# A reciprocal root on GpSimd, three chunks turned through DRAM, and a first tile on two queues

## The chip, the cores and the metric

The kernel runs on one core of one Trainium2 chip. Five engines work side by side in a core: TensorE (PE: matmuls and transposes, which write the PSUM banks; its weight loads are shown as PEld), VectorE (DVE), ScalarE (ACT), GpSimd (POOL) and SyncE (SP, which here issues the DMAs). Each engine takes its own instructions in order, and semaphores tie them together. The metric is the device time of one launch in microseconds.

## The reference

The input x is 2048 rows of 640 columns. Two parts follow each other, each with a layer norm ahead and a residual sum behind:

```python
def _layernorm(x, axis=-1, eps=1e-5):
    m = jnp.mean(x, axis=axis, keepdims=True)
    v = jnp.var(x, axis=axis, keepdims=True)
    return (x - m) / jnp.sqrt(v + eps)

h = x + _A_ref(_layernorm(x, axis=-1), A_wqkv, A_wo)
h2 = h + _B_ref(_layernorm(h, axis=-1), B_w_gate, B_w_up, B_w_down)
```

`_A_ref` is an attention with 32 heads of 20 columns in which every position sees itself and seven earlier ones at a distance of 2, 4, ... 14: `x @ wqkv` (640 x 1920), softmax over the 8 logits, the weighted sum of values, then `@ wo` (640 x 640). `_B_ref` is `(silu(x @ w_gate) * (x @ w_up)) @ w_down` with 1728 inner columns.

## The kernel before, in words

**Tiling.** The rows are taken in 4 blocks of 512, each held as 128 partitions by 4 row groups (`j`) of 640 columns. Every float32 matrix is split into a high part in the matmul's reduced type and a low remainder, and each product is made of three passes (high by high, high by low, low by high). So each operand costs an ACT copy for the high part and a VectorE subtraction for the low one.

**Stages.** `ln1` normalises a block's rows and turns them into columns, `qkv` multiplies them by the attention weights (480 columns at a time, four groups `g`) and writes queries, keys and values to DRAM; the scale of each row is applied as ACT empties the bank (L585). `att_load`, `att_qk`, `att_exp` and `att_av` do the attention of one block and group, nearly all of it on VectorE (L629, L636, L664, L672), and send the turned output to DRAM. `wo` multiplies by the output weights (L827), adds x and takes the second norm's statistics; `ln2_columns` turns the rows again (for blocks 0 to 2 the first half through DRAM, in `turn_pair`, and the second by TensorE, in `pair_columns`, L447 to L450). `ffn` runs 14 chunks of the feed-forward weights for blocks 0 and 1: `load_ffn` brings the weights into one of two raw buffers, `proj` (L899) makes gate and up, `gate` the product, `down` (L910) adds into five banks. Blocks 2 and 3 share some of their products (`early`, `pair`, `closing`; L994). The stages overlap: matmuls of one block run while VectorE does the attention of another.

**The norm's deviation.** `LnStats.rstd(j, n)` turns variances into 1/sqrt(var + eps) for n row groups at once. ACT takes the square root (L410; this needs another function table than the exponential and the silu, and a load of it shows as ACT_TABLE_LOAD), and VectorE makes the reciprocal and one Newton step in five or six instructions on 1 to 4 columns (L403 to L409, the last one makes the row bias). It is called 14 times: four times for block 0's first norm, once for each of the other three, twice for the second norm of blocks 0, 1 and 2, and once for that of block 3. `apply` and `apply_pair` then scale the rows on ACT.

**The end of a block.** `finish` adds the five banks of the down product to the rows and stores them. Four banks hold columns 0 to 511 of one row group each. The fifth holds columns 512 to 639 of all four row groups, the wrong way round: ACT copies it out (L1197), TensorE turns it in four transposes (L1201), VectorE adds it (L1212). It is called five times: for blocks 0 and 1, for block 2's first part (not stored), for block 3, and for block 2's second part at the very end.

**The start.** SP loads row groups of block 0's x one at a time (L514) and the attention weights (L553) in the planner's order. TensorE runs ten filler matmuls (`warm`, L497) from the start. For each row group VectorE takes mean and variance and subtracts the mean (`one_dve`, L390 to L392), TensorE turns it in five transposes (L541), and ACT and VectorE split it.

**The order.** Nothing is issued where it stands in the code. `P.add(engine, cost, function, reads, writes, priority)` collects some 2,700 operations, each of one or several instructions. `Plan.order` lists them by estimated costs and priorities (`PR`), then again in several rounds (`ROUNDS`) by due times that follow from TensorE's order. At the end the estimated start of each operation, plus a correction by its number (`SHIFT`), is the key of a last topological sort, and the functions are called in that order. The numbers of operations shift when operations are added or removed.

**On GpSimd** run a few memsets and, for 12 of the 16 attention groups, one sum (L690 and L692), of which the first instruction is there to wait: it reads the product that VectorE's L629 writes, so that the large sum starts when VectorE begins the one-input reduction L636.

Of the kernel before, what the change touches and what calls it, by code (L numbers as in the profile page):

```python
# [10 lines left out]
F32 = mybir.dt.float32  # L11
# [14 lines left out]
LOADED = (1, 2)  # L26
TURN = (3,)
# [3 lines left out]
EPS = 1e-5  # L31
# [5 lines left out]
ROUNDS = ((1.0, 20, 1.5), (1.5, 10, 3.5), (1.1, 0, 1.5), (1.4, 20, 3.5), (1.3, 3, 2.5), (1.2, 3, 2.5), (1.3, 20, 5.0),)  # L37
PR = {'g1': 0.6, 'y1': 0.6, 'x': 0.5, 'yst': 8, 'yld': 2, 'wqd': 4, 'wqh': 0.5, 'wql': 4, 'qev': 1, 'kvs': 0.4, 'atl': 1.2, 'exp': 0.5, 'ost': 3, 'wod': 2, 'woh': 8, 'wol': 1.2, 'old': 1.5, 'fld': 4, 'lst': 6, 'wev': 1.5, 'fh': 2.2, 'fl': 8, 'ln1': 8, 't1': 1, 'wo0': 1.2, 'wo': 2.2, 'ln1t': 1.2, 'xb': 0.4, 'tr': 10, 't1t': 2.2, 'ln1d': 0.5, 'hst': 10, 'hld': 10, 'ht': 1, 'hc': 2, 'jd': 3, 'jp': 8, 'js': 4, 'jl': 0.4, 'ja': 0.5, 'jfld': 1.2, 'jfh': 4, 'jfl': 1, 'jhi': 4, 'jmu': 0.4, 'jlo': 0.9, 'jcm': 0.5, 'w3': 1, 'w3e': 8, 'w3o': 0.4, 'w3x': 8, 'w3l': 2.2, 'jy': 6}

SHIFT = {  # L40
# [161 lines left out]
def program(tc, x_in, wqkv_in, wo_in, ffn_in, ffl_in, const_in, out):  # L202
# [7 lines left out]
    with tc.tile_pool(name="sb", bufs=1) as sb, tc.tile_pool(  # L210
# [51 lines left out]
        zsc = dr.tile([NB, D, 4, 64], F32, name="zsc")  # L262
        msc = dr.tile([6, 2, 128, 512], F32, name="msc")
# [19 lines left out]
        EPSC, BN, MV, RS1 = LN + 120, LN + 80, LN + 92, LN + 100  # L283
# [5 lines left out]
        def f(o, n):  # L289
            return fa[:, o : o + n]  # L290
# [16 lines left out]
        P.add("DVE", 0.2, lambda: V.memset(f(EPSC, 1), EPS), w=[rf(EPSC, 1)], prio=0)  # L307
        P.add("ACT", 0.1, lambda: A.activation(f(LN + 119, 1), f(EPSC, 1), AF.Sqrt), r=[rf(EPSC, 1)], w=[rf(LN + 119, 1)], prio=0, table="sqrt")
# [15 lines left out]
        class LnStats:  # L324
# [41 lines left out]
            def apply_pair(self, j):  # L366
                o = lambda: f(XN, 1280).rearrange("p (f j t) -> p f j t", j=2, t=32)[:, :, j, :]
                P.add("ACT", 0.95, lambda: A.activation(o(), self.src(j).rearrange("p (f t) -> p f t", t=32), AF.Identity, bias=f(self.NB + j, 1), scale=f(self.RS + j, 1)),
                      r=[self.srcr(j), rf(self.NB + j, 1), rf(self.RS + j, 1)], w=[rf(XN, 1280)], prio=self.prio)

            def one_bn(self, j):
# [9 lines left out]
                P.add("DVE", 1.45, bn, r=[self.srcr(j)], w=[rf(BN, 12), rf(MV + 2 * j, 2), rf(self.NEG + j, 1)], prio=self.prio)  # L381

# [12 lines left out]
            def rstd(self, j, n, after=()):  # L395
                STD, RS, TM, NEG, NB = (o + j for o in (self.STD, self.RS, self.TM, self.NEG, self.NB))
# [3 lines left out]
                fold = self.RS == self.SUM + 16  # L400

                def newton():
                    V.tensor_scalar(f(TM, n), var, sc, EPS, op0=ALU.mult, op1=ALU.add)  # L403
# [4 lines left out]
                    if fold:  # L408
                        V.tensor_mul(f(NB, n), f(NEG, n), f(RS, n))  # L409
# [966 lines left out]
```

## Time and profile before

| | |
|---|---|
| median of 3 runs | 844.13 us (843.86 to 844.89) |
| the profiled execution's own time | 841.39 us |
| its span, first to last instruction | 839.3 us |
| granted TensorE clock, mean | 0.999 |
| TensorE busy | 831.4 us, 99% of the span |
| VectorE busy | 694.7 us, 83% |
| ACT busy | 414.0 us, 49% |
| GpSimd busy | 23.2 us, 3% |

The profile is one execution. Its page gives busy times of the engines; further views give them by stretches of time, by groups of instructions (line, engine, operation, out<-in, shapes, count, then busy time and mean ns of one, then the idle time ahead of them and what ended it), the list of who waited for whom, the chain of work that ended last, and the instructions in order of time (start in us, length in us, then the instruction). In the latter, a mark in brackets is the engine's idle time before the instruction and what ended it. In rows of DMA issues the last number is the median time from issue to landing. "SPq" is SP's queue issuing a DMA.

### The profile page before, as it was taken

Reading aid. Unit: us, or ns where it says so; the run is one execution under the profiler, and the core shown is the slowest. Engines: PE = TensorE matmul, PEld = TensorE weight load, DVE = VectorE, ACT = ScalarE, POOL = GpSimd, SP = SyncE. Lnnn points to the kernel's source line nnn. Section 1 sums busy time; section 2 is a strip of 40 time slices with the busy share of each in tenths; the row PEclk is TensorE's granted clock in tenths of the full one; section 3 lists DMA queues with packets and bytes.
Section 4 is the critical chain, followed back from the end, with each engine's and each line's share of the span. In section 5 each row is a group of like instructions: output and inputs, shape, how many; then the busy total and the mean of one; then the engine's idle time right before and its main releaser. Section 6 shows DMA issues by size and latency. Waiting matters only on the chain.

```text
span 839.3 us, 10718 instructions
## 1 busy us (share of the span) xinstructions
PE 831.4 (99%) x3903; PEld 705.0 (84%) x3903; DVE 694.7 (83%) x823; ACT 414.0 (49%) x694; POOL 23.2 (3%) x33
## 2 busy tenths in 40 slices
PE   8999999999999999999999999999999999999998
PEld 7888888889978889888888988888887888888886
DVE  8599999999999999999999999996327866655552
ACT  7755853333763445755443486464465533323231
POOL 0000000000000000000000000000000000000000
PEclk9999999999999999999999999999999999999999
DMA  8996786568688687669898658787587644454441
GB/s 265 331 367 219 284 272 216 185 213 307 197 304 263 224 289 258 212 210 372 287 365 289 233 174 304 250 269 268 156 264 270 218 170 137 136 169 144 154 133 71
DMA packets 101796, 198.32 MB, mean 236 GB/s; under 512 B 35744, under 2 KB 61152, under 8 KB 101104
## 3 DMA queue, kind: packets, MB, share of 16 engines
q1 hardware_dynamic: 101744, 197.65, 69.6%
q8 instruction: 30, 0.49, 0.2%
q14 instruction: 22, 0.18, 0.1%
HBM read 147.87 MB, written 49.75 MB: 235 GB/s over the span
## 4 chain that ended last, share of the span: by engine, by line
PE 75%; DVE 15%; DMA 4%; issue 2%; ACT 2%; SPq 1%; DVEq 0%; ACTq 0%
PE bank L580 20%; PE bank L910 17%; PE bank L899 17%; PE bank L994 16%; PE bank L827 5%; DVE fa L629 2%; DVE fa L636 2%; DVE fa L672 2%; DVE fa L664 2%; DMA fa<-ysc 1%; DMA fa<-in_ffn_dram 1%; DMA ysc<-fa 1%; DVE fa L934 1%; DMA fa<-in_wqkv_dram 1%; DMA fa<-osc 1%
## 5 line engine op out<-in xcount | busy, mean ns | idle before, releaser
L899 PE MATMUL bank<-shb,ra 128*128 128x512 f32 x810 | 189.7, 390 | 1.1 <-DVE shb L450 1.1
L899 PEld LDWEIGHTS bank<-shb,ra 128*128 128x128 f32 x810 | 151.4, 188 | 32.4 <-DVE shb L450 1.5
L910 PE MATMUL bank<-ra,acts 128*128 128x512 f32 (+1 forms) x662 | 161.9, 389 | 0.2 <-DVE acts L945 0.2
L910 PEld LDWEIGHTS bank<-ra,acts 128*128 128x128 f32 x662 | 122.6, 188 | 25.5 <-DVE acts L945 0.5
L580 PE MATMUL bank<-ra,sha 128*128 128x480 f32 x480 | 105.1, 379 | 0.6 <-ACT sha L543 0.6
L580 PE MATMUL bank<-ra,shb 128*128 128x480 f32 x470 | 102.5, 378 | 0.0
L580 PEld LDWEIGHTS bank<-ra,sha 128*128 128x128 f32 x480 | 89.8, 188 | 14.5 <-ACT sha L543 0.9
L580 PEld LDWEIGHTS bank<-ra,shb 128*128 128x128 f32 x470 | 88.1, 188 | 13.2
L664 DVE TENSOR_TENSOR fa<-fa 128x2560 f32<-128x2560 f32 x32 | 90.2, 2820 | 0.6
L629 DVE TENSOR_TENSOR fa<-fa 128x2560 f32<-128x2560 f32 x32 | 90.1, 2816 | 0.8 <-DMA fa<-ksc 0.4
L636 DVE TENSOR_REDUCE fa<-fa 128x128 f32<-128x2560 f32 x32 | 90.0, 2814 | 0.4
L994 PE MATMUL bank<-shb,ra 128*128 128x512 f32 x360 | 86.8, 390 | 0.3 <-DVE fa L938 0.3
L1137 DVE TENSOR_TENSOR fa<-bank,fa 128x512 f32<-128x512 f32 x60 | 41.1, 691 | 52.8 <-PE bank L994 51.4
L994 PEld LDWEIGHTS bank<-shb,ra 128*128 128x128 f32 x360 | 67.2, 188 | 14.6 <-DVE fa L938 0.7
L672 DVE TENSOR_TENSOR fa<-fa 128x1280 f32<-128x1280 f32 (+2 forms) x70 | 76.7, 1095 | 1.1
L827 PE MATMUL bank<-ra 128*128 128x320 f32 x480 | 75.0, 310 | 0.0
L827 PEld LDWEIGHTS bank<-ra 128*128 128x128 f32 x480 | 72.1, 188 | 2.9 <-ACT fa L830 1.3
L585 ACT ACTIVATE st<-bank,fa 128x480 f32<-128x480 f32 x64 | 41.9, 656 | 57.2 <-PE bank L580 54.4
L994 PE MATMUL bank<-ra 128*128 128x512 f32 x288 | 68.2, 389 | 0.0
L944 ACT CAST acts<-fa 128x512 fp32r<-128x512 f32 x47 | 29.1, 620 | 71.9 <-DVE fa L934 50.3
L994 PEld LDWEIGHTS bank<-ra 128*128 128x128 f32 x288 | 54.1, 188 | 11.2
L876 ACT CAST ra<-fa 128x1280 fp32r<-128x1280 f32 (+1 forms) x38 | 45.8, 1205 | 24.1 <-PE bank L899 15.0
(146 smaller groups left out, 834.5 us busy)
## 6 DMA issues: line engine op xcount, KB each, us to landing
fa<-in_ffn_dram SPq DMA_DIRECT2D x46, 960.0 KB, 6.5
ra<-lsc SPq DMA_DIRECT2D x45, 320.0 KB, 3.0
fa<-ksc SPq DMA_DIRECT2D x16, 880.0 KB, 6.0
fa<-vsc SPq DMA_DIRECT2D x16, 880.0 KB, 6.9
ra<-lsc SPq DMA_DIRECT2D x21, 640.0 KB, 5.0
lsc<-ra SPq DMA_DIRECT2D x13, 640.0 KB, 3.2
ksc<-st SPq DMA_DIRECT2D x16, 320.0 KB, 2.8
qsc<-st SPq DMA_DIRECT2D x16, 320.0 KB, 3.6
```

Of the source, the lines that this page charges most:

```text
L580: T.matmul(banks[bk][:, 0:480], l, r_(wq(g, w, c), 480), start=(p, c) == first_mm, stop=(p, c) == last_mm)
L585: P.add("ACT", act(480) + 0.06, lambda bk=bk, j=j: A.activation(stage_t()[:, so : so + 1920].rearrange("p (t j c) -> p t j c", t=3, j=NJ)[ ...
L629: P.add("DVE", dve(2560), lambda: V.tensor_tensor(f(PROD, 2560).rearrange("p (j w c) -> p j w c", j=2, w=W), window(ko, 2 * jp), f(qo + 32 ...
L636: P.add("DVE", dve(2560), lambda: V.tensor_reduce(f(lo + 128 * jp, 128), f(PROD, 2560).rearrange("p (n d) -> p n d", d=DH), axis=AX.X, op= ...
L664: V.tensor_tensor(f(PROD, 2560).rearrange("p (j w d) -> p j w d", j=2, d=DH), bass.AP(tensor=fa[:, vo : vo + 160].tensor, offset=fa[:, vo ...
L672: V.tensor_add(dst(v), v[:, :, 0:m, :], v[:, :, m : 2 * m, :])
L827: T.matmul(banks[bk][:, 0:320], l, r_(m, 320), start=p == 0 and c == 0, stop=p == 2 and c == NC - 1)
L876: P.add("ACT", act(n), lambda: A.copy(r_(gu, n), f(raw, n)), r=[rf(raw, n)], w=[rr(gu, n)], prio=PR["fh"])
L899: T.matmul(banks[bk], r_(gu + 1280 * w + wid * c + col, 128), x2(a, c), start=p == 0 and c == 0, stop=p == 2 and c == NC - 1)
L910: T.matmul(banks[bk][:, lo:hi], l, m, start=first and p == 0, stop=last and p == len(passes) - 1)
L994: T.matmul(banks[bk], r_(ws[w] + 256 * q, 128), x(a, c), start=start and p == n == q == 0, stop=stop and p == 2 and n == len(terms) - 1 an ...
L1137: dv(0, lambda: V.tensor_add(fb(h, dst), banks[bk], fb(h, src)), [pb(bk)] + fr(h, src), fr(h, dst))
```

## The change

Four things are changed together.

- `rstd` becomes one operation of two GpSimd instructions: variance times a factor plus eps, then that to the power -0.5, whose exponent lies in a column filled by a memset. The square root on ACT, its first table load, and the Newton step on VectorE go. The row bias, minus mean times deviation, is now made on ACT beside each scaled row (`scaled`), 16 times.
- `finish` turns the last chunk of blocks 0, 1 and 3 (`FLAT`) by a VectorE transpose in 32x32 squares, one store to DRAM and four loads that put the squares in place. The unstored call for block 2 copies its chunk to LG as it is, and the last call adds that copy before the turn, which stays with TensorE. The very last row group's stores go out in halves on SP and ACT.
- Block 0's first row group is loaded in two halves, on SP and on ACT. Its mean is summed by ACT (256 columns) and VectorE (384 columns), the mean is subtracted from the first 128 columns and then from the other 512, and the five transposes go as one and four into banks 7 and 6.
- `ROUNDS` has nine rounds in place of seven, and `SHIFT` moves 194 operations (57 before). By the new numbers 10 is the first load of attention weights, 31 and 32 are the two subtractions of the first mean, 34 to 39 the first row group's transposes and splits, and 1008 and 1011 are two of the three subtractions at L450 for block 0.

```diff
-ROUNDS = ((1.0, 20, 1.5), (1.5, 10, 3.5), (1.1, 0, 1.5), (1.4, 20, 3.5), (1.3, 3, 2.5), (1.2, 3, 2.5), (1.3, 20, 5.0),)
+ROUNDS = ((1.5, 10, 3.5), (1.0, 6, 1.5), (1.3, 0, 5.0), (1.3, 6, 3.5), (1.4, 3, 1.5), (1.5, 20, 5.0), (1.2, 10, 1.5), (1.4, 10, 1.5), (1.0, 3, 5.0),)
 SHIFT = {
...
+    0: 12.6, 10: -198.4, 19: 2, 31: -245, 32: -195.6, 33: -1.9, 34: -118.2, 35: -103.5, 36: -91.6, 37: -90.6,
...
+    -0.3, 240: 10.4, 247: 19.9, 255: -2.7, 263: -30.3, 276: -18.9, 285: 9.2, 288: 26.8, 298: -9, 306: 6.9, 313:
...
+    928: 45.4, 932: -5.8, 940: 10.7, 942: -27.6, 958: -25.3, 979: -0.3, 986: -25.8, 1008: -26.1, 1011: -47,
...
-        P.add("DVE", 0.2, lambda: V.memset(f(EPSC, 1), EPS), w=[rf(EPSC, 1)], prio=0)
-        P.add("ACT", 0.1, lambda: A.activation(f(LN + 119, 1), f(EPSC, 1), AF.Sqrt), r=[rf(EPSC, 1)], w=[rf(LN + 119, 1)], prio=0, table="sqrt")
+        P.add("POOL", 0.1, lambda: G.memset(f(POW, 1), -0.5), w=[rf(POW, 1)], prio=0)
...
+            def one_split(self, j, cut=384):
+                src, xo = self.src(j), XN + 640 * j
+                P.add("ACT", 0.6, lambda: A.activation(f(xo + cut, 640 - cut), src[:, cut:640], AF.Identity, accum_out=f(self.SUM + j, 1)),
...
+                def mean():
+                    V.tensor_reduce(f(self.NEG + j, 1), src[:, 0:cut], axis=AX.X, op=ALU.add)
+                    V.tensor_scalar(f(self.NEG + j, 1), f(self.NEG + j, 1), f(self.SUM + j, 1), 1.0 / D, op0=ALU.add, op1=ALU.mult)
...
+                for o, e in ((0, 128), (128, 640)):
+                    P.add("DVE", 0.155 + 0.0006 * (e - o), lambda o=o, e=e: V.tensor_scalar(f(xo + o, e - o), src[:, o:e], f(self.NEG + j, 1), None, op0=ALU.subtract),
...
-                def newton():
-                    V.tensor_scalar(f(TM, n), var, sc, EPS, op0=ALU.mult, op1=ALU.add)
-                    V.reciprocal(f(RS, n), f(STD, n))
...
-                P.add("ACT", 0.3, lambda: A.activation(f(STD, n), var, AF.Sqrt, bias=f(EPSC, 1), scale=sc), r=[vr, rf(EPSC, 1), *after], w=[rf(STD, n)], prio=self.prio, table="sqrt")
...
+                def power():
+                    G.tensor_scalar(f(TM, n), var, sc, EPS, op0=ALU.mult, op1=ALU.add)
+                    G.tensor_tensor(f(RS, n), f(TM, n), f(POW, 1).to_broadcast([128, n]), op=ALU.pow)
+                P.add("POOL", 0.9, power, r=[vr, rf(POW, 1), *after], w=[rf(RS, n), rf(TM, n)], prio=self.prio)
...
+            def scaled(self, j, o, i, w):
+                NEG, RS, NB = (f(q + j, 1) for q in (self.NEG, self.RS, self.NB))
+
+                def rows():
+                    A.mul(NB, NEG, RS)
+                    A.activation(o(), i(), AF.Identity, bias=NB, scale=RS)
...
+            if js == (0,):
+                for a, (eng, E) in enumerate((("SP", Q), ("ACT", A))):
+                    P.add(eng, 0.4, lambda a=a, E=E: E.dma_start(
+                        fa[a:128:2, XR : XR + 640],
+                        x_in[0, 64 * a : 64 * a + 64, 0, :]), w=[("xh", a, a + 1)] if a else [rf(XR, 640)], prio=0, nbytes=nb(64, 2560))
...
-                (st.one_dve if j < 3 else st.one)(j)
-                for c0, n, bk, bo in ((0, 4, 7 - j % 2, 0), (4, 1, 5, j)):
+                (st.one_split if j == 0 else st.one_dve if j < 3 else st.one)(j)
+                for c0, n, bk, bo in ((0, 1, 7, 0), (1, 4, 6, 0)) if j == 0 else ((0, 4, 7 - j % 2, 0), (4, 1, 5, j)):
...
+            so = SIL if b == 2 else AB2 if b < 2 else XN + 2048
+            if not store:
+                P.add("ACT", act(512), lambda: A.copy(f(LG, 512), banks[d4]), r=[pb(d4)], w=[rf(LG, 512)], prio=0)
+            elif b == 2:
+                P.add("DVE", dve(512), lambda: V.tensor_add(f(so, 512), banks[d4], f(LG, 512)), r=[pb(d4), rf(LG, 512)], w=[rf(so, 512)], prio=0)
...
+            if store and b in FLAT:
+                cols, ckey = (lambda: f(so, 512)), rf(so, 512)
+                P.add("DVE", dve(512), lambda: V.transpose(f(so, 512), f(so, 512)), r=[ckey], w=[ckey], prio=PR["dt"])
+                P.add("SP", 0.45, lambda: Q.dma_start(dsc[b], f(so, 512)), r=[ckey], w=[(f"D{b}", 0, 4)], prio=PR["dt"], nbytes=nb(128, 2048))
+                for q in range(4):
+                    P.add("SP", 0.65, lambda q=q: Q.dma_start(
+                        fa[32 * q : 32 * q + 32, so : so + 512].rearrange("t (j d c) -> t j d c", j=NJ, d=4),
+                        dsc[b].rearrange("(d t) (j q c) -> q t j d c", t=32, j=NJ, q=4)[q]),
+                        r=[(f"D{b}", 0, 4)], w=[(f"T{b}", q, q + 1)] if q else [ckey], prio=PR["dt"], nbytes=nb(512, 128))
...
+                    if final and j == NJ - 1:
+                        for a, (eng, E) in enumerate((("SP", Q), ("ACT", A))):
+                            P.add(eng, 0.4, lambda row=row, o=o, e=e, a=a, E=E: E.dma_start(out[b, 64 * a : 64 * a + 64, NJ - 1, o:e], row()[a:128:2]), r=[key], prio=3, nbytes=nb(64, 4 * (e - o)))
```

More of the change, by code (lines that the diff above doesn't have):

```diff
@@ L419, in apply @@
                     i = lambda j: self.src(j).rearrange("p (f t) -> p f t", t=32)
-                P.add("ACT", 0.95, lambda: A.activation(o, i(j), AF.Identity, bias=f(self.NB + j, 1), scale=f(self.RS + j, 1)),
-                      r=[self.srcr(j), rf(self.NB + j, 1), rf(self.RS + j, 1)], w=[rf(XN, 2560) if self.turned else rf(xo, 640)], prio=self.prio)
+                self.scaled(j, lambda: o, lambda: i(j), rf(XN, 2560) if self.turned else rf(xo, 640))
+            def scaled(self, j, o, i, w):
[3 more added lines that the diff above has]
+                    A.activation(o(), i(), AF.Identity, bias=NB, scale=RS)
+                P.add("ACT", 1.2, rows, r=[self.srcr(j), rf(self.NEG + j, 1), rf(self.RS + j, 1)], w=[w, rf(self.NB + j, 1)], prio=self.prio)
         def turn_pair(b):
```

49 lines of the change are left out of this document (26 added, 23 removed), and 24 rows, old and new, of the table SHIFT.

## The prediction

> **What bounds the kernel now.** I read the page's first part, then the busy time by stretches, then the list of who waited for whom on TensorE.
>
> ```profile
> span 839.3 us, 10718 instructions
> PE 831.4 (99%) x3903; PEld 705.0 (84%) x3903; DVE 694.7 (83%) x823; ACT 414.0 (49%) x694; POOL 23.2 (3%) x33
> ```
>
> ```profile
> 0.00:10.00 10.00, 7.60 (x29) 5.77 (x30) 6.75 (x15) 4.96 (x10) 1.17 (x7) 1.00 0.76 249
> 10.00:230.00 220.00, 220.00 (x1063) 193.47 (x1062) 203.54 (x221) 123.06 (x245) 6.88 (x8) 1.00 0.77 260
> 230.00:240.00 10.00, 8.91 (x45) 7.17 (x45) 9.97 (x12) 8.34 (x13) 1.72 (x2) 1.00 0.80 297
> 240.00:830.00 590.00, 589.26 (x2741) 493.92 (x2740) 470.55 (x572) 277.63 (x428) 13.42 (x16) 1.00 0.68 228
> 830.00:839.30 9.30, 5.65 (x31) 4.69 (x30) 3.89 (x7) 0.00 (x0) 0.00 (x0) 0.91 0.36 141
> ```
>
> ```profile
> PE bank L497 <- POOL ra L1239: 1.3, 1, 1.3
> PE bank L899 <- DVE shb L450: 1.1, 1, 1.1
> ```
>
> The columns of the stretches are PE, PEld, DVE, ACT, POOL, then the granted clock. A busy matmul engine need not run at its best, so a second view is wanted, the chain of work in order of time:
>
> ```profile
> 13.86 165.46 PE bank L580 x766
> 254.17 6.80 PE bank L899 x30
> 260.97 3.40 PE bank L910 x15
> ```
>
> The chain has long runs of nothing but matmuls, 0.216 us apart at 480 columns (165.46 / 766) and 0.227 at 512 (6.80 / 30), at a granted clock of 1.00. So TensorE really is the bound. It idles 839.3 - 831.4 = 7.9 us: 2.4 in the first 10, 1.1 where block 0 is handed to the feed-forward stage (L450), 0.7 in the 590 us behind that, and 3.65 at the end. This decides how the parts are priced: work taken from ACT, VectorE or GpSimd is worth nothing unless one of those 7.9 us waits for it; work taken from TensorE is worth its whole length; and a new wait of TensorE costs its whole length, since there are no gaps to take it up.
>
> **The change, part by part.** *The turned chunk.* `finish` is called five times, each with one group of four TensorE transposes (L1201). Three (blocks 0, 1, 3) now turn on VectorE and through DRAM, and one (block 2's first, unstored) keeps its chunk unturned in LG. Four groups go, one stays.
>
> ```profile
> 394.53 0.60 PE L1201 MATMUL bank<-fa 128*128 128x128 f32 x4
> 394.88 0.48 PE L899 MATMUL bank<-shb,ra 128*128 128x512 f32 x1
> 812.64 0.66 PE L1201 MATMUL bank<-fa 128*128 128x128 f32 x4
> 813.05 0.47 PE L910 MATMUL bank<-ra,acts 128*128 128x512 f32 x1
> ```
>
> From the first transpose to the next matmul pass 0.35 and 0.41 us, so four groups are worth 1.4 to 1.6 us: take 1.5. This is the surest term, since matmuls stand on either side.
>
> In their place come, for each of three blocks, a VectorE transpose of 128x512, one store and four loads, all on SP's queue.
>
> ```profile
> L702 DVE STREAM_TRANSPOSE fa<-fa 128x320 f32<-128x320 f32 x30 | 15.2, 505 | 0.1
> L424 DVE STREAM_TRANSPOSE fa<-fa 128x1280 f32<-128x1280 f32 x3 | 4.5, 1503 | 0.9 <-ACT fa L368 0.9
> zsc<-fa SPq DMA_DIRECT2D x12, 160.0 KB, 4.0
> fa<-zsc SPq DMA_DIRECT2D x3, 640.0 KB, 5.8
> fa<-in_ffn_dram SPq DMA_DIRECT2D x46, 960.0 KB, 6.5
> ```
>
> By a line through the two transposes, 512 columns take 0.70 us; three are 2.1 us of VectorE, beside matmuls (the unstored call drops one addition). The DRAM round is 4.0 + 5.8 = 9.8 us by the nearest store and load. Only the last columns' addition and the output stores wait for it, nothing of TensorE. It does hold SP: the four loads wait for the store's landing, and what is queued behind them, weight loads above all, waits too, up to 4.0 us for each block. A weight load lands after 6.5 us, and a chunk of weights feeds TensorE for 6.80 + 3.40 = 10.2 us with two buffers in turn; that cover of 3.7 us and more hides most of the 4.0. I cost it at nothing; without the cover it would be three times up to 4.0, that is 12.0. In the block 3 case it runs within the last 25 us, where the output must only land before the end.
>
> *The deviations.* Fourteen times, ACT's square root and VectorE's five or six small steps become two GpSimd instructions, a multiply-add and a power.
>
> ```profile
> L410 ACT ACT_TABLE_LOAD x8 | 10.3, 1283 | 0.1
> L410 ACT ACTIVATE fa<-fa 128x2 f32<-128x2 f32 (+2 forms) x14 | 3.8, 293 | 0.9 <-DVE fa L379 0.8
> 228.47 0.16 DVE L403 TENSOR_SCALAR fa<-fa 128x2 f32<-128x2 f32 x1
> 229.32 0.16 DVE L409 TENSOR_TENSOR fa<-fa 128x2 f32<-128x2 f32 x1
> L353 ACT ACTIVATE fa<-fa 128x1 f32<-128x1 f32 x13 | 2.6, 203 | 0.4
> ```
>
> ACT loses 10.3 + 3.8 = 14.1 us and perhaps as many table loads again that bring the other function back; it gains sixteen products of 0.2 us (the row bias, made beside each application), 3.2 us. VectorE loses about 229.48 - 228.47 = 1.0 us fourteen times, 14 us. ACT is half idle and VectorE hides behind TensorE, so this counts only at the hand-overs. No row shows a power. The rows nearest in kind are GpSimd's two-input ones:
>
> ```profile
> L690 POOL TENSOR_TENSOR fa<-fa x12: 194/194/511, 79.2 to 541.6; 128x1 f32<-128x1 f32 x12
> L692 POOL TENSOR_TENSOR fa<-fa 128x640 f32<-128x640 f32 x12 | 18.9, 1575 | 0.0
> 346.86 0.68 DVE L945 TENSOR_TENSOR acts<-fa,acts 128x512 fp32r<-128x512 f32 x1
> 347.08 0.51 POOL L690 TENSOR_TENSOR fa<-fa 128x1 f32<-128x1 f32 x1 [72.75 <-DVE fa L629]
> ```
>
> So each of the two takes 0.19 to 1.58 us, the pair 0.4 to 3.2; by width (1 to 4 columns) it is nearest to the low end, and since a power is more than a product I take 1.0 for the pair. It replaces 0.29 + 1.0, or 2.6 where a table load of 1.28 stands ahead: no loss by itself, a gain of 1.6 at best. But the last two rows show a trap. L690 normally takes 194 ns; begun while VectorE's L945 with two inputs ran, it ended only with it, after 510. In the kernel before, that instruction waits for VectorE's L629, so that the sum behind it runs beside a one-input reduction. The new pair has no such gate.
>
> The Trainium skill says the same ("SBUF — State Buffer", section "SBUF: two separate sides"): VectorE with two SBUF inputs and GpSimd reading SBUF hold one port pair by exclusive lock, for a whole instruction. The trace agrees (510 against 194 ns). By that rule the pair could wait twice for a 2.8 us instruction and the gain would turn into the loss of the first rival below; by the 194 ns row alone there is no wait.
>
> Where it matters is the hand-over at 235 us:
>
> ```profile
> 230.82 2.82 DVE L629 TENSOR_TENSOR fa<-fa 128x2560 f32<-128x2560 f32 x1
> 236.41 0.41 DVE L450 TENSOR_TENSOR shb<-bank,shb 128x256 fp32r<-128x256 f32 x1
> ```
>
> TensorE's 1.1 us there wait for L450, which stands behind 5.6 us of attention on VectorE (236.41 - 230.82). Two of the new shifts move L450 operations earlier by 26.1 and 47.0 us of planner's key, ahead of such work, and VectorE is 1.0 us lighter just before. Best -1.1; at worst the pair waits out two L629-like instructions, +5.6. I take -0.5, near the small end, because the attention work, not the deviation, is what L450 waits behind.
>
> *The first tile.* Its halves go out on SP and ACT; the first weight load is moved ahead on SP; the tile's mean is shared by ACT and VectorE, and its first 128 columns are turned alone.
>
> ```profile
> 0.74 1.32 SPq L514 DMA_DIRECT2D fa<-in_x_dram  x2
> 1.32 4.16 PE L497 MATMUL bank<-ra 128*128 128x512 f32 x10 [1.32 <-POOL ra L1239]
> 6.01 0.74 PE L541 MATMUL bank<-fa 128*128 128x128 f32 x5 [0.53 <-DVE fa L392]
> 6.40 0.59 ACT L554 CAST ra<-fa 128x480 fp32r<-128x480 f32 x1 [4.16 <-DMA fa<-in_wqkv_dram]
> 6.50 0.47 PE L497 MATMUL bank<-ra 128*128 128x512 f32 x1
> 7.53 0.49 PE L580 MATMUL bank<-ra,sha 128*128 128x480 f32 x1 [0.55 <-ACT sha L543]
> ```
>
> Ten filler matmuls end at 1.32 + 4.16 = 5.48 and keep their place, so the first transpose can come 0.53 earlier at best. That wait of 0.53, the wait of 0.55 at 7.53 and the filler of 0.47 at 6.50 are the whole prize: 1.6. Against it, the first half of the tile now stands behind a weight load on SP, and one issue there takes 0.66 (1.32 / 2): a loss of 0.7. Weights that land before the tile's mean take the wait of 6.40 out, so I take -0.9, between the ends and nearer to the prize.
>
> The Trainium skill ("DMA: Bandwidth & Descriptors", section "Issuing engines are not separate DMA queues") says that issuing from several engines saves only the sequencer's issue time; by it the split alone is worth at most one 0.66 issue. No run here shows it yet.
>
> *The end.* The last addition ends at 836.11 and the span 3.2 later.
>
> ```profile
> 835.51 1.19 SPq L1217 DMA_DIRECT2D out_dram<-h  x2
> 835.69 0.42 DVE L1209 TENSOR_TENSOR h<-bank,h 128x256 f32<-128x256 f32 x1 [0.21 <-PE bank L910]
> ```
>
> Half-sized stores on two queues shorten at most part of one issue, about 0.6 (1.19 / 2): between -0.3 and +0.1, take -0.1.
>
> *The moved operations* touch all engines and the whole list, and the planner's rounds are new, so the order is new everywhere. Before, all of the main 820 us (10 to 830) hold 1.1 + 0.7 = 1.8 us of TensorE's waits: the most that a better order can save, while a worse one has no floor. Beyond the hand-over I take 0.
>
> **Sum.** -1.5 - 0.9 - 0.5 - 0.1 = -3.0 us. The profiled execution took 841.39 us with a span of 839.3, so it would be 838.4; the median of the runs, 844.13, lies 2.7 above that execution, and the same step from it gives 841.1. The best case is -1.6 - 1.6 - 1.8 - 0.3 = -5.3: 838.8. About 0.2% (1.7 us) is what a measurement tells from no change: faster is below 842.4, slower above 845.8.
>
> **The rivals.** *The power is held up by VectorE (slower).* The mechanism is the 510 ns row. Two hand-overs may have no cover: the one at 235 us, and one of those further on that make up the 0.7 us. If the pair waits out one 2.8 us instruction at each, TensorE waits 5.6 more, and the 0.5 is not won: 841.1 + 0.5 + 5.6 = 847.2. For it: two-input operations fill much of VectorE's attention time, and GpSimd's queue is in order, with the sums of 1.58 in it. Against it: the old path of up to 2.6 us goes away. It decides from 4.7 us of added waits.
>
> *The new order gives the gain back (no change).* Waits of 0.5 to 1.1 us, like those at 6.01, 7.53 and 236, appear in three to six of the reordered places, 3 us in all: 844.1. For it: 0.7 us of waits in 590 is hard to keep. Against it: VectorE has 14 us less to do.
>
> *SP is held (slower or none).* Were the weight loads uncovered once, +4.0: 845.1; three times, +12.0: 853.1. Against it: a cover of 3.7 us and a second buffer.
>
> *The tile comes no earlier (faster still).* Without the 0.9: 842.0.
>
> **How the numbers follow.** The forecast with its variant of the late tile has 0.62, own range 838.8 to 842.4; the order that gives all back, 0.13, and SP held once, 0.03, both within 0.2%; the held-up power, 0.13; a worse order or SP held more often, 0.09, above 846. So faster 0.62, same 0.16, slower 0.22. The range 838.8 to 847.0 leaves out part of the last two cases and a few hundredths below.
>
> **What would show it.** Right: `finish` has 4 transposes in place of 20; no table load for a root; first real matmul before 7.53; TensorE's wait for L450 under 1.1; and TensorE's idle time, 7.9, down by about 1.5 with busy time down as well. Wrong: GpSimd's two new instructions longer than 1.6 us or ending with a VectorE one, ACT's application of a row waiting for them, and new TensorE waits over 1 us, at the hand-overs or for weights.

## The result and the profile after

The changed kernel is slower. Six runs gave a median of 851.1 us (850.53 to 854.27); the kernel before ran beside it at 843.72 (841.95 to 844.89). The ratio is 1.0101, 95% interval 1.0079 to 1.0123. A second measurement, told below, gave 1.0085 (1.0066 to 1.0104). So the change costs 7 to 8.5 us, where 3 us less was forecast.

The profiled execution took 854.27 us, 3.2 above the median; its span is 852.5 us. From the page, the span and the busy time of each engine:

```profile
span 852.5 us, 10632 instructions
PE 835.4 (98%) x3887; PEld 706.7 (83%) x3887; DVE 690.4 (81%) x748; ACT 392.1 (46%) x679; POOL 46.5 (5%) x62
```

The work went as announced: 16 matmuls fewer (3903 to 3887, the four groups of transposes), VectorE 4.3 us lighter, ACT 21.9 lighter, GpSimd 23.3 busier. But TensorE's idle time went from 7.9 to 17.1 us, and it is busy 4 us longer although it has less to do. The busy time by stretches (PE, PEld, DVE, ACT, POOL, granted clock, DMA share, GB/s) shows where:

```profile
0.00:10.00 10.00, 6.00 (x17) 4.04 (x17) 4.87 (x12) 4.53 (x10) 1.20 (x8) 0.93 0.79 270
230.00:240.00 10.00, 9.31 (x44) 7.75 (x42) 10.00 (x7) 5.77 (x17) 4.04 (x4) 1.00 0.61 220
240.00:840.00 600.00, 592.15 (x2734) 494.90 (x2735) 471.52 (x551) 271.64 (x435) 21.51 (x26) 1.00 0.68 229
840.00:852.50 12.50, 8.03 (x43) 6.66 (x42) 4.81 (x8) 0.00 (x0) 0.00 (x0) 0.97 0.31 118
```

Before, the 590 us behind the hand-over held 0.7 us of waits; now the stretch of 600 us holds 7.9. Of these, 3.3 us are still the hand-over itself, which came late into this stretch (1.82, 0.70 and 0.75 us, at 241 to 244 us), so about 4.6 lie behind it. TensorE's list of waits (who waited for whom: us in total, times, longest) names them:

```profile
PE bank L476 <- ACT fa L449: 2.5, 2, 1.8
PE bank L934 <- DMA ra<-lsc: 2.2, 1, 2.2
PE bank L576 <- DVE fa L422: 1.4, 1, 1.4
PE bank L1029 <- ACT fa L1066: 1.3, 1, 1.3
PE bank L862 <- ACT fa L865: 1.2, 2, 0.8
PE bank L576 <- DVE fa L408: 1.2, 1, 1.2
```

L476 and L449 are the transposes and the row scaling of block 0's second norm (the hand-over), L576 the transposes of the first row groups (the start), the DMA one a load of weights' low parts at 463 us. The start of some matmuls, read from the order of time in several profiles (us; the last two columns are runs told below):

| start of the | before | after | pair runs alone | with the start in the old order and the table first as well |
|---|---|---|---|---|
| first attention product | 7.53 | 11.05 | 11.36 | 7.52 |
| last of the 960 products with the attention weights | 235.41 | 238.94 | 238.73 | 235.84 |
| first gate/up product | 236.88 | 244.12 | 241.82 | 239.07 |
| 60th gate/up product | 250.38 | 259.22 | 255.31 | 252.57 |
| last matmul | 835.37 | 847.75 | 840.96 | 840.09 |

The start is 3.5 us late, and the hand-over adds 5.3 more by the 60th gate/up product; a further 3.5 comes behind it in this execution, but only 0.7 in a second profiled one (848.7 us of span), whose waits at the start and at the hand-over are nearly the same.

**The start.** From the order of time (start, length, instruction; in brackets the idle time before it and what ended it):

```profile
4.34 1.28 ACT L400 ACT_TABLE_LOAD   x1 [4.34 <-DMA fa<-in_x_dram]
5.64 0.42 ACT L400 ACTIVATE fa<-fa 128x256 f32<-128x256 f32 x1
6.18 0.21 DVE L405 TENSOR_SCALAR fa<-fa 128x1 f32<-128x1 f32 x1 [1.26 <-ACT fa L400]
6.86 0.96 PE L576 MATMUL bank<-fa 128*128 128x128 f32 x5 [1.22 <-DVE fa L408]
9.47 1.93 PE L576 MATMUL bank<-fa 128*128 128x128 f32 x6 [1.42 <-DVE fa L422]
```

The removed square root of a constant had brought a function table in before any data came. Now the first activation that needs one is ACT's part of the tile's sum, and the load of 1.28 us stands between the landed tile and its mean. The first transposes come at 6.86 us (6.01 before). Then the new order puts the second row group's transposes (9.47) ahead of the first product (11.05). Of the 3.5 us, the table accounts for 1.3: with it loaded first, in a run below, the first product comes at 9.72. Some 2.2 us remain against the 7.53 of before, and the transposes put ahead are what the trace shows there.

**The hand-over.** The pair of GpSimd instructions at 212 us, for the first half of block 0's second norm:

```profile
211.90 2.83 DVE L699 TENSOR_TENSOR fa<-fa 128x2560 f32<-128x2560 f32 x1
212.12 2.65 POOL L432 TENSOR_SCALAR fa<-fa 128x2 f32<-128x2 f32 x1 [12.69 <-ACT fa L373]
214.76 1.49 DVE L707 TENSOR_TENSOR fa<-fa 128x1280 f32<-128x1280 f32 x1
214.86 1.96 POOL L433 TENSOR_TENSOR fa<-fa 128x2 f32<-128x2 f32 x1
216.85 0.29 ACT L448 ACTIVATE fa<-fa 128x1 f32<-128x1 f32 x1 [4.26 <-POOL fa L433]
219.57 0.43 DVE L852 TENSOR_TENSOR ra<-fa,ra 128x256 fp32r<-128x256 f32 x1 [3.31 <-ACT ra L851]
```

The first instruction ends with the VectorE one beside it (214.77 and 214.73 us), which has two inputs. The second is held too, and ends 0.57 us behind its neighbour (216.82 and 216.25), nearly the 0.70 that it takes alone. That makes 4.7 us from start to end for two columns. ACT, whose queue is in order, waits 4.26 us for the deviation; a weight split behind it (L851) is late; and VectorE, which needs that, stands idle for 3.31 us. What VectorE does next is late too, the second half of the norm with it: its multiply-add below starts at 237.91 us, and at 235.61 in the run with the pair free, 2.3 earlier.

```profile
237.91 0.64 POOL L432 TENSOR_SCALAR fa<-fa 128x2 f32<-128x2 f32 x1 [4.03 <-ACT fa L373]
238.64 1.16 POOL L433 TENSOR_TENSOR fa<-fa 128x2 f32<-128x2 f32 x1
241.14 0.44 PE L476 MATMUL bank<-fa 128*128 128x128 f32 x2 [1.82 <-ACT fa L449]
244.12 4.12 PE L934 MATMUL bank<-shb,ra 128*128 128x512 f32 x10 [0.75 <-ACT shb L478]
```

TensorE has run out of attention products by then. And it pays twice: the last row has ten products in 4.12 us, 0.41 apart instead of 0.227, and the first 60 take 15.1 us (244.12 to 259.22) where they took 13.5. The stretches around it and at the start show why (same columns):

```profile
239.00:242.00 3.00, 0.75 (x4) 0.20 (x2) 3.00 (x3) 2.15 (x5) 0.80 (x1) 1.00 0.71 231
245.00:248.00 3.00, 3.00 (x9) 2.33 (x9) 3.00 (x7) 3.00 (x6) 0.00 (x0) 0.58 0.22 80
9.00:12.00 3.00, 2.41 (x9) 1.98 (x10) 2.93 (x7) 2.46 (x7) 0.00 (x0) 0.50 0.95 348
12.00:15.00 3.00, 3.00 (x11) 2.50 (x10) 3.00 (x8) 3.00 (x9) 0.00 (x0) 0.50 0.56 163
```

A stretch in which TensorE worked 0.75 us of 3 is followed by one at a granted clock of 0.58; at the start it is 0.50 for 6 us. Between the last attention product (to 239.31 us) and the first gate/up product (244.12) TensorE ran ten transposes and no product for 4.8 us. With the pair alone, in a run below, this gap is 2.7 us (239.11 to 241.82), and the clock stays at 1.00. The Trainium skill ("TensorE: Matmul & The Clock Gate", section "Part 1: The HAM clock gate") gives a half-rate clock after at least one idle window of about 3.4 us. The trace agrees on the half rate (0.50). Here TensorE wasn't idle so long at a stretch: no single wait is above 1.82 us. Whether transposes count as work for the clock, no run here settles; at the start filler matmuls ran among them too.

### The profile page after: what moved, and what is told of

It reads as the page before. It is cut to its first block, busy times and chain, and to the rows that moved or that the text cites. A ratio compares the mean times of both kernels' runs of the same rounds, so it can differ in the third digit from the quotient of the medians.

```text
span 852.5 us, 10632 instructions
## 1 busy us (share of the span) xinstructions
PE 835.4 (98%) x3887; PEld 706.7 (83%) x3887; DVE 690.4 (81%) x748; ACT 392.1 (46%) x679; POOL 46.5 (5%) x62
## 4 chain that ended last, share of the span: by engine, by line
PE 42%; DMA 5%; DVE 1%; SPq 1%; issue 1%; ACT 0%; DVEq 0%; ACTq 0%
PE bank L1029 16%; PE bank L945 14%; PE bank L934 6%; PE bank L862 4%; PE bank L1051 2%; DMA fa<-osc 1%; DMA fa<-ysc 1%; DMA out_dram<-h 1%; DMA fa<-dsc 1%; DMA ysc<-fa 0%; DVE fa L707 0%; DVE fa L664 0%; SPq L486 0%; SPq L1244 0%; SPq L1067 0%
```

## The experiments

Each ran beside the kernel before on the same chip, and ratios are to that. All but the unaltered repetition issue their operations by a written list (`order = P.ranked(RANK)` in place of `order = P.order()`), taken from one of the two kernels, so that an edit doesn't shuffle the rest. "Old order" is the list of the kernel before, "new order" that of the changed one; in the edits, [old order] and [new order] stand for these lists.

**One part alone, in the old order.** *The power:*

```diff
-P.add("ACT", 0.3, ... A.activation(f(STD, n), var, AF.Sqrt, bias=f(EPSC, 1), scale=sc)); newton()
+P.add("POOL", 0.9, power, ...)
```

> The kernel before, in its own order, with only the deviation moved to GpSimd as a multiply-add and a power in the place of the square root; the row bias is made on ACT. If VectorE's two-input instructions hold the pair wherever it stands (theory one), the hand-overs lose 3 to 8 us: 846 to 851. If the pair is harmless and only the new order exposes it (theory two), the lighter VectorE and ACT give 842 to 844.

842.43 us against 843.58, ratio 0.9986 (0.9975 to 0.9997): 1.2 us faster. The change of engine is no loss by itself.

*The first tile:*

```diff
-(st.one_dve if j < 3 else st.one)(j)
+(st.one_split if j == 0 else st.one_dve if j < 3 else st.one)(j)
+# with its two loads, on SP and ACT, and its transposes as one and four
```

> The kernel before, in its own order, with only the new first tile: two halves on SP and ACT, the mean shared by ACT and VectorE, transposes as one and four. Its early dummy square root stays, so ACT has its table before the tile lands. If the late start of the changed kernel comes from the table load that fell on the tile's sum (theory one), this is 0.5 to 1 us faster than before: 842.5 to 843. If splitting the tile costs by itself (theory two), it is 1 us slower or more: 844.5 to 848.

843.41, ratio 1.0000 (0.9989 to 1.0012): nothing. The tile's sum is ready earlier and the first transposes come at 5.21 us instead of 6.01, but TensorE then waits for the weights. Their load is issued at 2.24 us here (2.10 before; 0.73 in the changed kernel, whose order moves it ahead), so this run tests the split of the tile alone. In the order of time:

```profile
5.21 0.96 PE L711 MATMUL bank<-fa 128*128 128x128 f32 x5
6.89 0.59 ACT L724 CAST ra<-fa 128x480 fp32r<-128x480 f32 x1 [2.52 <-DMA fa<-in_wqkv_dram]
7.70 0.48 PE L750 MATMUL bank<-ra,sha 128*128 128x480 f32 x1 [1.30 <-ACT sha L713]
```

*The end of a block:* the new `finish`, whose loads were placed 4 us behind the store and the addition 7 us behind those.

```diff
+FLAT = (0, 1, 3)
-def finish(...): ...   # TensorE turns
+def finish(...): ...   # through DRAM, the copy in LG, split stores
```

> The kernel before, in its own order, with only the new end of the blocks: three chunks turned by VectorE through DRAM, block 2's first chunk unturned in LG, split last stores. TensorE loses four groups of transposes of 0.36 us: 842 (theory one). If SP is held by the loads that wait for the store, or the split stores end later, it is 844 to 848 (theory two).

847.31, ratio 1.0046 (1.0033 to 1.0058): 3.9 us slower. SP's queue tells why. The load of the next block's keys (`fa<-ksc`) is issued at 413.76 us in the kernel before; here, behind the four loads of the turn (2.69 us of issue from 402.69) and the output stores that wait for them, at 418.99. Rows of this run:

```profile
402.69 2.69 SPq L1373 DMA_DIRECT2D fa<-dsc  x4
411.81 3.29 SPq L1401 DMA_DIRECT2D out_dram<-h  x4
418.99 0.60 SPq L783 DMA_DIRECT2D fa<-ksc  x1
428.68 2.83 DVE L793 TENSOR_TENSOR fa<-fa 128x2560 f32<-128x2560 f32 x1 [2.75 <-DMA fa<-ksc]
432.16 0.72 PE L1074 MATMUL bank<-acts,ra 128*128 128x512 f32 x2 [1.32 <-DVE acts L1109]
```

VectorE stands 2.75 us for the keys, the gate's product behind it is late, and TensorE waits 1.32 us. It is one of five new waits of 0.6 to 1.5 us, between 214 and 586 us, 5.3 in all; the others weren't traced back this far, and the one at 214 us lies ahead of the first turn. The loads' places were written by hand, and others weren't tried.

*All three parts:*

```diff
-RANK = [new order]
+RANK = [old order]
```

> All three parts of the change (power on GpSimd, first tile on two queues, three last chunks turned through DRAM with the copy in LG and the split stores), issued in the kernel before's order. Alone in that order they gave -1.2, 0.0 and +3.7 us. If the parts add up and the rest of the 7.5 us is the new order: 843.6 + 2.5 = 846.1, between 845 and 847.5, with the first product of block 0's feed-forward within 1.5 us of the last attention product. If the parts disturb each other whatever the order: 849 to 852.

846.72 against 843.08, ratio 1.0046 (1.0024 to 1.0068): 3.9 us slower; the single parts sum to 2.7. In the old order, then, the parts cost about half of the 7 to 8.5 us. That split doesn't carry over to the new order, where the turn's 3.9 isn't found again (below).

**One part undone, in the new order.** *The square root and the Newton step again:*

```diff
-P.add("POOL", 0.9, power, ...)
+P.add("ACT", 0.3, ... AF.Sqrt ...); P.add("DVE", 1.2, newton, ...)
```

> The changed kernel with only the deviation put back on ACT and VectorE, all other operations in their new order. Theory one, with the GpSimd pair held by VectorE at the hand-over at 235 us: the 4 us that are lost there by the two traces come back, 846 to 848 us. Theory two: no gain, 850 to 852; TensorE's wait behind the row scaling stays.

868.43, ratio 1.0300 (1.0275 to 1.0326): 17 us slower than the changed kernel. The largest wait of TensorE is now

```profile
PE bank L612 <- ACT fa L585: 10.6, 3, 5.7
```

since the Newton step stands on VectorE behind the attention that this order puts ahead: at the hand-over the square root is done at 239.8 us, a reduction of 2.81 us (L807) follows on VectorE from 240.66, and the Newton step begins at 244.40. The new order needs the deviation to be off VectorE; this run says nothing on what the power itself costs.

*All parts undone, the unturned copy and the split stores apart:*

```diff
-FLAT = (0, 1, 3)
+FLAT = ()
# and the square root, the Newton step and the first tile as in the kernel before
```

> The changed kernel with three of its parts undone (square root and Newton step as before, first tile by one load and one statistics pass, TensorE turning all three chunks); what stays is the new order of all operations, block 2's unturned chunk in LG and the split last stores. If the parts cost the time (theory one), it comes near the kernel before: 842 to 846 us. If the moved operations cost it (theory two), it stays at 849 or more.

871.71, ratio 1.0330 (1.0302 to 1.0358), with the same 10.6 us of waits. For that reason it doesn't price the order.

*The old first tile:*

```diff
-(st.one_split if j == 0 else st.one_dve if j < 3 else st.one)(j)
+(st.one_dve if j < 3 else st.one)(j)
```

> The changed kernel with only the first tile put back: one load on SP, mean and variance on VectorE, four and one transposes. By the two traces the 60th attention matmul starts 4.8 us later after the change (26.93 against 22.15). Theory one: 3 to 5 us come back, 846 to 848. If the start is lost through the order of the loads (theory two), at most 1 us, 850.

853.88, ratio 1.0120 (1.0090 to 1.0150): 1.6 to 3 us above the changed kernel, with intervals that overlap. The split is no harm by itself in this order either.

*TensorE turns all chunks again:*

```diff
-FLAT = (0, 1, 3)
+FLAT = ()
```

> The changed kernel with TensorE turning the chunks of blocks 0, 1 and 3 again (three groups of transposes, 0.36 us each). If turning through DRAM only took work from TensorE, this is 1.1 us slower: 852. If its loads hold SP's queue, the wait of 2.2 us for a weight load at 460 us goes and it is 1 us faster or more: 848 to 850.

850.51, ratio 1.0081 (1.0058 to 1.0105): within 1 us of the changed kernel. What costs 3.9 us in the old order can't be measured in the new one.

*The function table loaded at the very start:*

```diff
+V.memset(f(LN + 121, 1), 0.0)
+A.activation(f(LN + 119, 1), f(LN + 121, 1), AF.Identity)
 order = P.ranked(RANK)
```

> The changed kernel with one dummy activation at the very start of ACT's work, as the kernel before had, so that the 1.28 us table load no longer stands between the landing of the first tile and its sum. Theory one: the first transposes come 1.3 us earlier, less filler is needed and TensorE keeps its clock: 847 to 849.8. Theory two, that the loads' order sets the start: 850.5 to 851.5.

850.27, ratio 1.0075 (1.0054 to 1.0095). The load goes to 0.72 us and the sum comes 1.46 earlier (4.18 instead of 5.64 us), the first product at 9.72 instead of 11.05; of that, 0.8 to 2.2 us arrive at the end, by the changed kernel's two ratios, and the intervals overlap.

**The held pair.** A tiny VectorE copy reads the first half's deviation and stands ahead of the 128x2560 product, so that the pair has the port for itself:

```diff
 stats.rstd(0, 2)
+if b == 0:
+    P.add("DVE", 0.1, lambda: V.tensor_copy(f(LN + 119, 1), f(stats.RS, 1)), r=[rf(stats.RS, 1)], ...)
```

> The changed kernel with one small VectorE copy added, which reads the first deviations of block 0's second norm and stands ahead of the product of 128x2560 that ran beside them: VectorE waits about 1.3 us there and the pair runs alone. If the pair's being held (2.65 and 1.96 us in place of 0.2 and 0.9, after which ACT's split and so VectorE come 3.3 us late) makes the hand-over late: multiply-add near 0.2, power near 0.9, the first product of block 0's feed-forward 2 to 3.3 us earlier, 848 to 849. If the order of the second half's work alone sets it: under 0.7 us, 850.4 to 851.1.

847.57 against 843.08, ratio 1.0049 (1.0031 to 1.0067): 3.5 us less than the changed kernel by the medians, 3.0 to 4.4 by its two ratios, from one added wait. The intervals just meet with one of its measurements (1.0066 to 1.0104) and are apart with the other (1.0079 to 1.0123). The order of time of this run, and a stretch behind its hand-over:

```profile
211.91 0.19 POOL L564 TENSOR_SCALAR fa<-fa 128x2 f32<-128x2 f32 x1 [12.70 <-ACT fa L505]
212.19 0.70 POOL L565 TENSOR_TENSOR fa<-fa 128x2 f32<-128x2 f32 x1
212.92 0.15 DVE L1011 COPY fa<-fa 128x1 f32<-128x1 f32 x1 [1.26 <-POOL fa L565]
213.00 2.83 DVE L831 TENSOR_TENSOR fa<-fa 128x2560 f32<-128x2560 f32 x1
```

```profile
242.00:245.00 3.00, 3.00 (x14) 2.46 (x14) 3.00 (x7) 3.00 (x5) 0.00 (x0) 1.00 0.50 194
```

0.19 and 0.70 us in place of 2.65 and 1.96. VectorE waits 1.26 us on purpose and saves the 3.31. The first gate/up product comes at 241.82 instead of 244.12, and the clock stays at 1.00: 3.9 us by the 60th, though the first attention product is no earlier (11.36). Trace and time agree: this is the largest piece.

**Which stretch of the order.** *The old order to about 250 us, the new one behind:*

```diff
-RANK = [new order]
+RANK = [old order up to place 760, then new order]
```

> All parts of the changed kernel; the first 760 operations (up to about 250 us) in the kernel before's order, the rest in the new order. If the new order loses its time at the start and at the hand-over to block 0's feed-forward (8.8 us in the profiles by the 60th gate or up product): 851.1 - 8.8 + about 1 for the parts in that stretch = 843.5, 842 to 845.5. If it loses it behind 250 us, or the stretches only shift the wait: 848 to 851.

851.09, ratio 1.0085 (1.0064 to 1.0106): no gain, against the expectation. The 60th gate/up product comes at 251.81, 7.4 us earlier than in the changed kernel; then TensorE waits 1.38 us up to 260.4 and 2.29 up to 266.6 for VectorE's steps of the gate (VectorE has attention of the new order to catch up with), and some 3 us more later on. A splice of two orders has a seam of its own, so it doesn't prove that the first 250 us are innocent.

*The old order for the first 28 us alone, and beside its repetition the changed kernel, unaltered:*

```diff
-RANK = [new order]
+RANK = [old order up to place 180, then new order]
```

> The changed kernel; its first 180 operations (up to about 28 us) in the kernel before's order, the rest in the new order. The profiles put the 60th attention product 4.8 us later than before in the new order and 2.1 us later with all parts in the old order. If a late start is passed on to the end: 851.1 - 2.7 = 848.4, 847 to 849.5. If the wait at the hand-over takes it up: 850.5 to 851.5.

> The changed kernel with its first 180 operations (28 us) in the kernel before's order, as once before. If a late start is passed on to the end, by the profiles' 2.5 us: the run before this one minus 2.5 (2.0 to 3.0). If the hand-over takes it up: less than 1 us under it.

> The changed kernel, unaltered, to be compared on one chip with the next run. By the first six runs: 851.1, 850.5 to 854.3, 7 to 9 us over the kernel before.

First 850.1 (ratio 1.0095, 1.0070 to 1.0119). In the second measurement 851.1 (1.0083, 1.0061 to 1.0106) beside 850.77 for the changed kernel (1.0085, 1.0066 to 1.0104). In that second profile the 60th attention product comes 1.9 us earlier than in the changed kernel's, the 60th gate/up product 0.65, the last matmul 0.3 later: the slow-clock stretch at the hand-over is longer, and the wait for the weights at 459 us is 1.8 instead of 1.0 us. An earlier start alone brings nothing measurable in this order.

*All mendings together:* the edits for the start, the table and the pair, with the turn by TensorE and then through DRAM.

```diff
-RANK = [new order]
+RANK = [old order up to place 180, then new order]
+A.activation(f(LN + 119, 1), f(LN + 121, 1), AF.Identity)
+    P.add("DVE", 0.1, lambda: V.tensor_copy(f(LN + 119, 1), f(stats.RS, 1)), ...)
-FLAT = (0, 1, 3)
+FLAT = ()          # the first of the two runs alone
```

> The changed kernel with its first 180 operations in the kernel before's order, the function table loaded ahead of the first tile, VectorE waiting for the first pair of block 0's second norm, and no chunk turned through DRAM. If these four are the whole loss: 851.1 - 2.7 - 3.5 - 0.6, and of the 0.8 of the table some 0.3, = 844.0, 842.5 to 845. If the rest of the new order costs time of its own: 846 to 848.

> The first 180 operations in the kernel before's order, the table loaded first and the first pair of block 0's second norm alone, as in the run of all four mendings (845.3, 2.6 us over the kernel before), but blocks 0, 1 and 3 turned through DRAM again. If the turn is hidden in the new order: within 1 us of that, 2 to 3.5 us over the kernel before. If it costs what it does in the old order: 6 to 7 us over.

845.27 (ratio 1.0031, 1.0018 to 1.0044) and 846.25 (1.0030, 1.0015 to 1.0046). So the turn through DRAM costs nothing that can be measured in the new order, against what it costs in the old one, and start and table together bring 1.6 us once the pair is free, with intervals that overlap. Some 2.5 us stay unexplained; the largest waits of the last run are

```profile
PE bank L994 <- ACT fa L997: 2.5, 3, 1.1
PE bank L1068 <- ACT shb L610: 0.8, 1, 0.8
```

that is, the products of the attention's output waiting for ACT to empty a bank, at 321, 462 and 466 us. Which of the moved operations does that was not tried.

**A version that is faster than both.** The old order with the power, the unturned copy in LG and the split stores; nothing through DRAM, the old first tile:

```diff
-FLAT = (0, 1, 3)
+FLAT = ()
-(st.one_split if j == 0 else st.one_dve if j < 3 else st.one)(j)
+(st.one_dve if j < 3 else st.one)(j)
-RANK = [new order]
+RANK = [old order]
```

> The kernel before's order with the power on GpSimd, the unturned copy of block 2's last chunk in LG and the split stores; the other chunks are turned by TensorE, nothing through DRAM. If the DRAM turn alone costs the 3.7 us of the run with the new end of a block: one group of transposes fewer than with the power alone (842.4), so 842.0, 841.6 to 842.6. If the copy and its late addition, or the split stores, cost some of it: 843 to 845.

841.02 against 843.08, ratio 0.9966 (0.9952 to 0.9980): 2.9 us faster than the kernel before by the ratio, 2.1 by the medians. The first half's pair is not held in this order: it runs at 210.53 us, where VectorE idles and then has a one-input reduction, in 0.19 and 0.70 us. The second half's power is held, 1.95 us at 229 us. So is the whole pair of block 1's second norm, beside two-input VectorE instructions:

```profile
340.12 4.20 POOL L563 TENSOR_SCALAR fa<-fa 128x2 f32<-128x2 f32 x1 [64.83 <-ACT fa L504]
344.41 3.29 POOL L564 TENSOR_TENSOR fa<-fa 128x2 f32<-128x2 f32 x1
```

With a waiting VectorE copy for the power at 229 us:

```diff
 stats.rstd(2, 2)
+if b == 0:
+    P.add("DVE", 0.1, lambda: V.tensor_copy(f(LN + 119, 1), f(stats.RS + 2, 1)), ...)
```

> The kernel before's order with the power on GpSimd, the copy in LG and the split stores, nothing turned through DRAM (841.0), and VectorE waiting for the second pair of block 0's second norm, so that the power isn't held (1.95 us there). If a held pair always costs its length: 839.5 to 840.0. If it costs only where later work of VectorE or TensorE hangs on it, since VectorE now waits too: 840.5 to 841.5.

842.63, ratio 0.9991 (0.9979 to 1.0002): the pair is free, and the time is about 2 us worse, with intervals that just meet. GpSimd's instructions without the copy, then with it:

```profile
228.79 0.21 POOL L563 TENSOR_SCALAR fa<-fa 128x2 f32<-128x2 f32 x1 [17.28 <-ACT fa L504]
229.08 1.95 POOL L564 TENSOR_TENSOR fa<-fa 128x2 f32<-128x2 f32 x1
```

```profile
228.74 0.70 POOL L564 TENSOR_TENSOR fa<-fa 128x2 f32<-128x2 f32 x1
229.47 0.15 DVE L1009 COPY fa<-fa 128x1 f32<-128x1 f32 x1 [0.87 <-POOL fa L564]
```

In the old order the second half of the norm comes 9 us ahead of where it comes in the changed kernel, and TensorE has attention products left meanwhile. So freeing the power has nothing to win there. In the profiles the first gate/up product comes at 238.40 us with the copy, after a wait of 1.49 for VectorE, and at 237.85 without; whether this wait is the 2 us isn't shown.

## Why the prediction was wrong

**Moved operations, "beyond the hand-over I take 0".** This step failed most widely. The order wasn't neutral; it took away the slack that the other terms were priced with. The nearest comparison has the power, the copy in LG, the split stores and the turn by TensorE in both: ratio 0.9966 in the old order, 1.0081 in the new one (which also has the split tile, worth 0.0 in the old order), 9.7 us apart. The second half of block 0's norm came 9.1 us later (237.91 against 228.79 us), so that no product was left to cover it. With start and pair mended it still starts at 232.86, and these 4.1 us are the order's own; of the rest the held pair made 2.3 and the late start about 2.5. The first half's pair, too, is held only where this order puts it, beside two-input attention. The text had written "a worse one has no floor" and gave that case 0.09. What remains after all mendings, 2.5 us over the kernel before and 5.5 over these parts in the old order (1.0031 against 0.9966), is of this kind too, as far as is known; its cause stays open.

**The deviations, "-0.5" at the hand-over.** The price of the pair was right: estimated 1.0 us, measured 0.19 + 0.70. The trap was seen as well: each instruction of the pair was held by about one VectorE instruction (2.65 + 1.96 us against 0.89), where the rival had 2.8 us for a whole hand-over. Its signs came, too: GpSimd's instruction over 1.6 us, and ACT's row scaling waiting for it. What failed is the weight. The rival asked for two hand-overs in which TensorE waits out an instruction, and "the old path of up to 2.6 us goes away" spoke against it. One pair was enough, and TensorE didn't wait for it at all: ACT did, 4.26 us, then VectorE, 3.31, and the hand-over 25 us later inherited that. The halved clock behind the wait added 1.6 us, which no term held. Freeing the pair gave about 3.5 us back. The pair can't be blamed alone: in the old order the first half's pair isn't held, and a kernel with the later holds, 1.25 us at 229 us and 6.6 at 340 us, is still faster than before. The run of the power alone (-1.2) is close to the term of -0.5.

**The first tile, "-0.9".** Alone it is 0.0, within ±1.0. The first transposes did come 0.8 us earlier, but the weights came no earlier in that run, and TensorE waited for them. In the changed kernel the weights are issued first, and ACT no longer waits for them, as "weights that land before the tile's mean" said. Yet the term became +3.5 in the trace. For 1.3 of it the prediction had no term. It booked the table loads of the square root as a gain and didn't ask what becomes of the one at the start, which wasn't removed but moved to the first activation. The other 2.2 stand where the new order puts the second row group's transposes ahead of the first product. That late start hardly reaches the end in the new order, though.

**The turned chunk, "-1.5", SP's hold "at nothing".** The four groups went (3903 to 3887 matmuls). The hold's cover was judged on weight loads. In the old order it was the attention's key load that stood behind the turn, and the end of a block cost +3.9 in all, where the forecast's terms for it make -1.6. That is 5.5 off, more than the "held once" case (+4.0 on top of the forecast). In the new order it cost nothing, and the gain of 1.5 can't be measured either: turning by TensorE again gave 850.51, within the interval.

**The end, "-0.1".** From the last matmul's start to the end it was 3.90 us and is 4.73 in both profiles of the changed kernel: +0.8. The split stores themselves are at most 0.1 of it, since runs with them in the old order take 3.95 to 4.01; the rest comes with the new order, in which the last two additions of 128x256 come together. The last stores, two on each of two queues:

```profile
848.53 1.13 SPq L1270 DMA_DIRECT2D out_dram<-h  x2
848.54 1.42 ACTq L1270 DMA_DIRECT2D out_dram<-h  x2
```

**The range** ended at 847.0. It held the held-up power and one held SP, each by itself, but no order that uncovers both the start and the hand-over.

## What to carry to other kernels

Price a moved step against the work that covers it in the new order, not in the old profile: a held GpSimd pair at one place cost about 3.5 us in the new order, while longer holds elsewhere left a kernel in the old order faster than before; the DRAM turn cost nothing measurable in the one and, with its loads placed by hand, 3.9 in the other. When small GpSimd steps go in beside a busy VectorE, follow the wait one engine further than the reader of the result: an in-order ACT queue handed it back to VectorE. And before removing an instruction that brings a function table in early, find the next instruction that will need it.

## What was not expected of the hardware

- A power on GpSimd takes 0.70 us for 128x2, where nothing holds it (the run with the pair alone). Beside a VectorE instruction with two inputs in SBUF, a 128x2 multiply-add took 2.65 us in place of 0.19.
- The granted clock fell to one half for about 3 us behind 4.8 us that held ten transposes and no product, and at the start for 6 us. Behind a gap of 2.7 us without a product it stayed at 1.00 (the run with the pair alone), and behind one of 2.8 us as well (the last of the runs with all mendings).
